# A gated linear recurrence and an ELU layer on one core: product 2 of the fast first layer and its bank's copy three products earlier, one ELU and some transfers one place later

## The chip, the core and the metric

The kernel runs on one core of a Trainium2 chip. The core has five engines that work side by side and wait for one another through semaphores: TensorE (in the profile PE, its weight loads PEld), VectorE (DVE), ScalarE (ACT), GpSimd (POOL) and SyncE (SP, which here only starts transfers). Each engine takes its instructions in the order in which the program emits them. TensorE writes its results into PSUM banks of 128x512 numbers of four bytes; DVE and ACT read them from there, and POOL cannot.

The metric is the device time of one execution in microseconds (us). Of the kernel before, three runs gave 630.42, 631.64 and 630.42 us, median 630.42 us.

## The reference

```python
def _attn_ref(q, k, v, a_re, a_im):           # each (4, 8, 768, 48)
    mag = np.sqrt(a_re * a_re + a_im * a_im)
    scale = np.minimum(mag, 0.999) / (mag + 1e-06)
    a_re_n, a_im_n = (a_re * scale, a_im * scale)
    for t in range(S):
        new_re = ar * S_re - ai * S_im        # ar, ai: row t of a_re_n, a_im_n
        new_im = ar * S_im + ai * S_re
        kv = np.einsum('bhd,bhe->bhde', k[:, :, t], v[:, :, t])
        S_re, S_im = (new_re + kv, new_im)
        y[:, :, t] = np.einsum('bhd,bhde->bhe', q[:, :, t], S_re)

def _moe_ref(x, w_in, w_out):                 # x (3072, 384), w_in (384, 2048), w_out (2048, 384)
    h = x @ w_in
    g = np.where(h > 0.0, h, np.exp(np.minimum(h, 0.0)) - 1.0)
    return g @ w_out
```

The output of the first function, with heads and their 48 columns side by side, is the `x` of the second: 4 sequences of 768 tokens, 384 columns, a hidden layer of 2048 with an ELU, and back to 384. The weights come in as double precision and are rounded on the chip.

## The kernel before

**Units.** The tokens are worked in 12 units, u = 0 to 11, each 128 tokens of two sequences. For a unit the kernel turns the gates into decays and angles (functions `squares` to `waves`), multiplies keys and queries by them (`scaled`, `gated`), transposes both, forms scores, carries the state (`small`, `masked`, `state_sums`, `valued_pe`, `carried_pe`), copies the result to `x` (`copied`, `seam`), and passes it through the two layers. Units 0 to 2 take the first layer as plain products (`inner`, `elu`); units 3 to 11 take it through a scheme with fewer products, described below. The second layer is seven products of halves (`product`) for all units from 2 on.

**The keys and queries of units 4 to 11** are turned by DVE's transpose in blocks of 32 (`flipped`, L1049) and then brought to their places by nine transfers of SP for the queries (`moved`, L1058, tile `qt<-kt`) and nine for the keys (`kt<-cs`), while POOL copies the blocks that stay on their partitions (`stayed`, L1066). The turned queries lie for that time in the tile `kt`, so the keys' transfers into `kt` come after the queries' have left it. `small` (L1221) then needs all of `kt`.

**The first layer of units 3 to 11** ("block u" below is the first layer of unit u) is 20 products p. Each is four matmuls of 128x128 by 128x128 (`mult`, L1539). In the order of TensorE:

`ORDER = 8, 1, 6, 3, 9, 7, 5, 0, 2, 14, 12, 10, 16, 18, 4, 17, 19, 13, 11, 15`

The products are summed in five PSUM banks, several after one another in the same bank: z takes 8, 1, 3, 16, 17, 15; w takes 6, 5, 14, 10, 4, 11; b takes 7; x takes 2, 12, 13; y takes 9, 0, 18, 19. Between two products of a bank its sum so far is needed, so an ACT copy (`kept`, L1552) or a DVE sum (`joint`, L1555) reads it, and the bank's next product waits for that reading:

- copy of x after product 2 into part '01' (`kept(u, '01', 'x')`): product 12 waits for it;
- copies of w after 6, 5 and 14 into '31', '30' and '10': products 5, 14 and 10 wait for them;
- copy of z after 1 into '21': product 3 waits for it; copy of x after 12 into '00': product 13;
- sum of '31' with z after product 3, and with b after product 7: product 16 waits for the first.

When a part is complete it gets its ELU: two ACT operations (`low`, L1560 and L1561), one DVE operation (`whole_of`, L1564). Part '31' is the first that is complete. While this goes on, ACT also takes two squares of a later unit's gates (`squares`, L727 and L728), DVE turns the next unit's queries and keys, and POOL multiplies that unit's keys by their gates (`gated`, L1011).

**The order of all this** is written out by hand up to unit 3 or so (the list `first`); after that every step has a due time in a plan (`put(at, fn, ...)`), and the plan is sorted by due time. Sixteen slots make a unit; the products of a block are 0.4 slots apart. The table `SHIFT` adds to a due time: an entry without `@` counts for every unit from 4 on, one with `@u` for unit u alone; in both the unit's number is left out of the name. Since an engine works in the order of emission, a shift matters only where the step passes another one of the same engine:

```python
    def put(at, fn, *args):
        at += shifted(fn, args)
```

Of the kernel before, what the change touches and what calls it, by code (L numbers as in the profile page):

```python
# [505 lines left out]
def kernel(  # L506
# [510 lines left out]
    PAIRED = 2  # L1017
# [353 lines left out]
    def folded(u, h, ks):  # L1371
        for k in ks:
            a, b, op = {
                3: (X(u, h, 0, 0), X(u, h, 1, 0), ALU.subtract),
                1: (X(u, h, 1, 0), X(u, h, 1, 1), ALU.add),
                2: (X(u, h, 1, 0), X(u, h, 0, 0), ALU.subtract),
                4: (X(u, h, 0, 1), X(u, h, 0, 0), ALU.subtract),
            }[k]
            nc.vector.tensor_tensor(out=S_of(u, k, h), in0=a, in1=b, op=op)  # L1379
# [250 lines left out]
    def warm(n):  # L1630
# [17 lines left out]
        "gated(None, ('k',))": 0.5, "gated(None, ('k',))@11": -0.3, "gated(None, ('k',))@5": -0.2,  # L1648
        "gated(None, ('q',))": 0.45, "gated(None, ('q',))@11": -0.2, "hidden(0,)": 0.05,
# [42 lines left out]
    }  # L1692

    def shifted(fn, args):

        alike = fn in (summed_in, combined, test, test_fetch) or not args
        u = 0 if alike else args[0] if type(args[0]) is int else args[-1]
        key = fn.__name__ + str(args if alike else args[1:])
        key = key.replace(repr(ALU.add), "+").replace(repr(ALU.subtract), "-")
        more = 0.0 if fn in (mult, product) or not (alike or u > PAIRED + 1) else SHIFT.get(key, 0.0)  # L1700
        return more + SHIFT.get(f"{key}@{u}", 0.0)
# [17 lines left out]
    def gates_of(u, *at):  # L1719
# [24 lines left out]
        (convert,), (waves, 1), (inner, 0, 2), (inner, 0, 0), (fetch, "in", 4), (fetch, "in", 5),  # L1744
        (load_a, 2), (table, "natural_log_exp_and_others", 1), (gated, 1, 0), (convert,),
# [12 lines left out]
        (fetch, "out", 5), *3 * [(convert,)], (load_v, 2), (powers, 2), (convert,), (elu, 1, 8),  # L1758
        (convert,), (elu, 0, 10), (convert,), (noted, 2), (ratios, 2), *3 * [(convert,)],
        (elu, 0, 14), (inner, 1, 10), *2 * [(convert,)], (elu, 0, 12), (convert,), (elu, 1, 10),  # L1760
        *4 * [(convert,)], (load_qk, 2), (convert,), (fetch, "out", 6), (project, 1, 0, 0, 4),
        (convert,), (inner, 1, 14), (slopes, 2), *3 * [(convert,)], (project, 1, 1, 0, 4),
        (project, 0, 0, 0, 4), (angles, 2), (lengths, 2), (fetch, "out", 7), (project, 0, 0, 4, 8),
        (elu, 1, 14), (project, 0, 1, 0, 4), (convert,), (decays, 2), (project, 1, 0, 4, 8),
        (carried, 2), *2 * [(convert,)], (table, "trig_and_small", 2), *2 * [(convert,)],
        (turns, 2), (waves, 2), (convert,), (table, "natural_log_exp_and_others", 2), (scaled, 2),
        (project, 0, 1, 4, 8), (convert,), (begun, 3), (convert,), (table, "trig_and_small", 3),
        (project, 0, 1, 8, 12), (convert,), (project, 1, 1, 4, 8), (squares, 3), (gated, 2),
        (project, 1, 0, 8, 12), *2 * [(convert,)], (joined, 3), (convert,), (transposed, 2, "k", 1),
        (transposed, 2, "q", 1), (convert,), (table, "natural_log_exp_and_others", 3), (convert,),  # L1770
        (ends, 2), (convert,), (logarithms, 3), (project, 1, 1, 8, 12), (powers, 3), (load_qk, 3),
        (transposed, 2, "k", 0), (convert,), (ratios, 3), (convert,), (lengths, 3),
        (project, 1, 0, 12, 16), (slopes, 3), (convert,), (transposed, 2, "q", 0),
        (project, 1, 1, 12, 16), (angles, 3), (scored, 2), (opened,), (states, 2, 0), (valued, 2),
        *3 * [(convert,)], (seam, 2), (project, 0, 0, 8, 12), (combined, 1, 1), (summed_in, 0),
        (noted, 3), (carried, 3), (summed_in, 1), (combined, 2, 1), (combined, 4, 1),
        (combined, 1, 0), (summed_in, 4), (summed_in, 2), (project, 0, 1, 12, 16), (combined, 2, 0),
        (turns, 3), (combined, 4, 0), (inner, 2, 4), (inner, 2, 6), (load_a, 4), (ends, 3),
        (inner, 2, 2), (load_v, 3), (inner, 2, 0), (elu, 2, 4), (scaled, 3), (elu, 2, 6),
        (summed_in, 3), (elu, 2, 2), (waves, 3), (gated, 3, None, ("k",)), (elu, 2, 0),  # L1780
        (gated, 3, None, ("q",)), (project, 0, 0, 12, 16), (inner, 2, 10), (transposed, 3, "k", 0),
        (warm, 2), (begun, 4), (folded, 2, 0, (3, 1)), (load_v, 4), (inner, 2, 8), (summed_in, 7),
        (squares, 4), (elu, 2, 10), (load_qk, 4), (transposed, 3, "q", 0), (transposed, 3, "q", 1),
# [154 lines left out]
```

## Time and profile before

| | |
|---|---|
| three runs, median | 630.42 us (630.42 to 631.64) |
| the profiled execution | 630.71 us |
| its span, first to last instruction | 628.9 us |
| TensorE busy | 605.8 us, 96% of the span |
| VectorE, ScalarE, GpSimd busy | 505.4, 415.0, 205.3 us |
| one product of the first layer, start to start | 0.89 us |

The span is shorter than the execution's own time by 1.81 us, which lie before the first and behind the last instruction. A row of the timeline reads: start and length in us, engine, line, operation, tile written<-tiles read, shapes, how many instructions were merged, and in brackets the idle time of the engine just before, with what ended it. A product of the first layer is eight TensorE records; its record is 1.06 us long though the next product starts 0.89 us after it, since matmuls are pipelined, so an idle time in brackets is shorter than the delay of the start.

### The profile page before, as it was taken

The page shows a single profiled execution, that of the slowest core. Times are in us where ns is not written, and L with a number is a line of the kernel's source. Part 1 is how long each engine was busy: PE and PEld are TensorE (multiplying, and loading weights), DVE is VectorE, ACT ScalarE, POOL GpSimd, SP SyncE. Part 2 cuts the span into 40 slices and gives each one's busy share as a digit, 9 for nine tenths or more (in the row PEclk, how much of TensorE's full clock was granted, in tenths as well). Part 3 has the DMA queues.
Part 4 walks back from the last instruction along what each step waited for, and adds up shares of the span by engine and source line. Part 5 has one row for each costly group of instructions (what it writes and reads, how often), then busy time and mean ns, then how long its engine had stood idle before and what let it go on. Part 6 is the DMA issues. An engine that isn't in the chain of part 4 may idle for free. (4 is left out here: it accounts for less than half of the span.)

```text
span 628.9 us, 16981 instructions
## 1 busy us (share of the span) xinstructions
PE 605.8 (96%) x6980; PEld 549.4 (87%) x6980; DVE 505.4 (80%) x789; ACT 415.0 (66%) x681; POOL 205.3 (33%) x248
## 2 busy tenths in 40 slices
PE   8889999999999999999999999999999999999996
PEld 5778886577899889999999988999999999999996
DVE  6999999877688988888888878879778877874482
ACT  6985573776868657677777776766767767661250
POOL 2010100103124624634734633634634633622000
PEclk9899999999999999999999999999999999999999
DMA  9988649541733355665565464574674675252101
GB/s 161 180 151 145 135 148 202 129 76 31 105 53 64 63 94 105 119 115 126 96 118 129 82 126 93 122 125 93 121 122 97 121 123 113 57 94 65 35 2 32
DMA packets 192179, 65.54 MB, mean 104 GB/s; under 512 B 168116, under 2 KB 181596, under 8 KB 192092
## 3 DMA queue, kind: packets, MB, share of 16 engines
q1 hardware_dynamic: 187920, 62.72, 52.1%
q0 software_dynamic: 3520, 1.20, 1.8%
q8 instruction: 57, 0.93, 0.6%
q10 hardware_dynamic: 652, 0.44, 0.3%
q14 instruction: 30, 0.25, 0.1%
HBM read 48.91 MB, written 4.80 MB: 85 GB/s over the span
## 5 line engine op out<-in xcount | busy, mean ns | idle before, releaser
L1401 PE MATMUL mlp<-w_out,g 128*128 128x192 f32 x640 | 111.9, 328 | 0.0
L1401 PEld LDWEIGHTS mlp<-w_out,g 128*128 128x128 f32 x640 | 104.3, 190 | 3.3 <-DVE ee L1415 0.6
L1123 POOL TENSOR_TENSOR S<-S,T 128x384 f32<-128x384 f32 x36 | 38.0, 1058 | 151.2 <-DVE S L1121 87.7
L1379 DVE TENSOR_TENSOR g<-g 128x512 f32<-128x512 f32 x80 | 60.7, 775 | 6.3 <-PE mlp L1401 4.7
L1292 PE MATMUL mlp<-x,w_in 128*128 128x256 f32 x288 | 64.0, 380 | 1.2 <-DMA x<-y 1.2
L1292 PEld LDWEIGHTS mlp<-x,w_in 128*128 128x128 f32 x288 | 54.2, 190 | 9.8 <-ACT n L850 1.8
L1560 ACT ACTIVATE ee<-g 128x512 f32<-128x512 f32 x63 | 39.5, 628 | 34.6 <-DVE g L1555 32.2
L1539 PE MATMUL mlp<-x,w_in 128*128 128x128 f32 x424 | 56.1, 275 | 0.0
L1272 POOL DMA_DIRECT2D x<-y x62 | 30.5, 498 | 73.6 <-ACT y L1168 41.3
L1401 PE MATMUL mlp<-w,g 128*128 128x192 f32 x320 | 54.5, 329 | 0.0
L1564 DVE SCALAR_TENSOR_TENSOR g<-ee,g 128x512 f32<-128x512 f32 x63 | 43.1, 693 | 13.1 <-ACT ee L1561 13.1
L1401 PEld LDWEIGHTS mlp<-w,g 128*128 128x128 f32 x320 | 51.8, 190 | 0.6
L1539 PEld LDWEIGHTS mlp<-x,w_in 128*128 128x128 f32 x424 | 51.6, 192 | 0.1
L1561 ACT ACTIVATE ee<-ee 128x512 f32<-128x512 f32 x72 | 45.4, 630 | 2.3
L1552 ACT COPY g<-mlp 128x512 f32<-128x512 f32 x36 | 21.0, 586 | 39.0 <-PE mlp L1539 39.0
L1555 DVE TENSOR_TENSOR g<-g,mlp 128x512 f32<-128x512 f32 x45 | 30.5, 677 | 16.1 <-PE mlp L1539 14.7
L1011 POOL TENSOR_TENSOR kg<-k,cs 128x1536 f32<-128x1536 f32 x8 | 36.9, 4614 | 1.7 <-POOL x L1522 1.4
L1539 PE MATMUL y<-x,w_in 128*128 128x128 f32 x216 | 29.4, 279 | 4.7 <-ACT g L1552 4.7
L1539 PEld LDWEIGHTS y<-x,w_in 128*128 128x128 f32 x216 | 26.2, 192 | 6.2 <-ACT g L1552 6.2
L1282 ACT ACT_TABLE_LOAD x24 | 30.8, 1283 | 0.5
L912 ACT ACTIVATE n<-w 64x384 f32<-64x384 f32 (+1 forms) x60 | 28.1, 486 | 3.9 <-PE w L897 3.0
L1539 PE MATMUL mlp<-x,g 128*128 128x128 f32 x224 | 29.7, 276 | 0.8 <-ACT g L1552 0.8
(220 smaller groups left out, 1368.0 us busy)
## 6 DMA issues: line engine op xcount, KB each, us to landing
w<-in_moe_w_out_dram SPq DMA_DIRECT2D x8, 768.0 KB, 5.9
g<-in_moe_w_in_dram SPq DMA_DIRECT2D x24, 256.0 KB, 3.7
g<-in_moe_w_out_dram SPq DMA_DIRECT2D x24, 256.0 KB, 2.8
w<-in_moe_w_in_dram SPq DMA_DIRECT2D x16, 288.0 KB, 4.8
vn<-in_v_dram SPq DMA_DIRECT2D x24, 192.0 KB, 3.8
qt<-kt SPq DMA_DIRECT2D x72, 64.0 KB, 3.4
kt<-cs SPq DMA_DIRECT2D x72, 64.0 KB, 2.5
q<-in_q_dram SPq DMA_DIRECT2D x11, 384.0 KB, 4.6
```

Of the source, the lines that this page charges most:

```text
L1011: eng.tensor_tensor(out=to.rearrange("p (h i d) -> p h i d", i=2, d=D), in0=each.unsqueeze(2).to_broadcast([C, step * H, 2, D]), in1=x["cs ...
L1123: eng.tensor_tensor(out=new_s, in0=new_s, in1=wide, op=ALU.mult)
L1272: eng.dma_start(out=x["x"][ds(j * HP + D, G), i], in_=x["y"][ds(j * HP + i * G, G)])
L1282: nc.scalar.preload_act_table_set(name)
L1292: nc.tensor.matmul(t[:, e], lhsT=w_in[:, i, ts(f + e, C)], rhs=x["x"][:, i], start=(i == 0), stop=(i == NI - 1),)
L1379: nc.vector.tensor_tensor(out=S_of(u, k, h), in0=a, in1=b, op=op)
L1401: nc.tensor.matmul(to, lhsT=a[:, m], rhs=b[:, m], start=(first and h == 0 and m == 0), stop=False, skip_group_check=True,)
L1539: nc.tensor.matmul(x["c" + c][:, ts(m, C)], lhsT=a[:, m], rhs=x["mix"][p], start=(p == BANKS[c][0] and m == 0), stop=False, skip_group_che ...
L1555: nc.vector.tensor_tensor(out=part(u, to), in0=part(u, a), in1=part(u, b), op=op)
L1560: nc.scalar.activation(out=e, in_=part(u, of), func=AF.Relu, scale=-1.0)
L1561: nc.scalar.activation(out=e, in_=e, func=AF.Exp, scale=-1.0)
L1564: nc.vector.scalar_tensor_tensor(out=part(u, to), in0=nat[u]["e", to], scalar=-1.0, in1=part(u, of), op0=ALU.add, op1=ALU.max,)
```

## The change

Nothing is computed differently; steps change places.

- **Product 2** in blocks 4 to 11 gets a shift of -1.2 slots: TensorE's order becomes 8, 1, 6, 3, 9, 7, **2**, 5, 0, 14, 12, 10 and on as before. To allow this, `shifted` now takes entries for `mult`.
- **The copy of bank x** into '01' gets -1.2 slots too: ACT's order in blocks 4 to 11 was copy '30', ELU of '31', copy '01', copy '10'; it becomes copy '01', copy '30', ELU of '31', copy '10'.
- **The sums and the ELU of '31'** get +0.4 slots in blocks 4 to 11 (one product). On DVE only one step passes another: the sum for '20' (reads bank y after product 0) now comes before the last step of the ELU of '31'.
- **In block 3** the copy '10' of bank w comes before the two squares of unit 5 on ACT, not behind them; the product order stays.
- **The queries' turning and transfers** get +0.3 slots: on DVE the last sum of the second layer (`product(u, 3, 1)`, L1427) now comes before the first of the two transposes, not between them. On SP nothing passes anything, except in block 9 (transfers of unit 10), where a shift of 2 slots puts one check fetch of a weight (`test_fetch`, 256 KB) ahead of the queries' nine transfers; on POOL the sum `joined` of unit 11 comes before unit 10's `stayed` queries there.
- **Early in the program** (the list `first`): the load of unit 2's gates comes before the fetch of a part of `w_in`, not behind it, on SP; and the two notes of unit 2 (`noted`, L807) come before two exponentials and two ELUs on ACT, not behind them.

```diff
@@ SHIFT
+        "flipped('q', 0)": 0.3,  "flipped('q', 1)": 0.3,
-        "joint('31', '31', 'z', -)": -0.5,
+        "joint('31', '31', 'b', +)": 0.4,  "joint('31', '31', 'z', -)": -0.1,
-        "kept('10', 'w')@3": 0.2,
+        "kept('01', 'x')": -1.2,
+        "load_a()@10": 0.05,
+        "low('31', '31')": 0.4,
-        "moved('k', 0)@10": 0.6,
+        "moved('k', 0)@10": 2.6,
+        "moved('q', 0)": 0.3,  "moved('q', 1)": 0.3,  "moved('q', 2)": 0.3,
+        "moved('q', 0)@10": 2,  "moved('q', 1)@10": 2,  "moved('q', 2)@10": 2,
+        "stayed('q',)@10": 2,
+        "mult(14,)@3": -0.2,  "mult(2,)": -1.2,
+        "whole_of('31', '31')": 0.4,  "whole_of('31', '31')@4": 0.3,
@@ shifted
-        more = 0.0 if fn in (mult, product) or not (alike or u > PAIRED + 1) else SHIFT.get(key, 0.0)
+        more = SHIFT.get(key, 0.0) if alike or u > PAIRED + 1 else 0.0
@@ first
-        ... (fetch, "in", 4), (fetch, "in", 5), (load_a, 2), ...
+        ... (fetch, "in", 4), (load_a, 2), (fetch, "in", 5), ...
-        ... (load_v, 2), (powers, 2), (convert,), (elu, 1, 8), (convert,), (elu, 0, 10), (convert,), (noted, 2), (ratios, 2), ...
+        ... (noted, 2), *2 * [(convert,)], (load_v, 2), (powers, 2), (convert,), (elu, 1, 8), (convert,), (elu, 0, 10), (convert,), (ratios, 2), ...
```

The diff is put together here by entry; in the file the table is sorted by name, so most of its lines move. The shifts of the keys' transfer of unit 10, of `load_a` and of product 14 in block 3 change no engine's order by themselves.

More of the change, by code (lines that the diff above doesn't have):

```diff
@@ L1642 @@
         "ends()@3": -0.5, "ends()@4": 0.1, "flipped('k', 0)": 0.3, "flipped('k', 0)@4": 0.1,
[5 rows of a table removed]
-        "gated(None, ('k',))": 0.5, "gated(None, ('k',))@11": -0.3, "gated(None, ('k',))@5": -0.2,
-        "gated(None, ('q',))": 0.45, "gated(None, ('q',))@11": -0.2, "hidden(0,)": 0.05,
[16 rows of a table removed]
[5 rows of a table added]
+        "folded(1, (4,))@5": -0.7, "gated()": 0.05, "gated(None, ('k',))": 0.5,
+        "gated(None, ('k',))@11": -0.3, "gated(None, ('k',))@5": -0.2, "gated(None, ('q',))": 0.45,
[19 rows of a table added]
         "powers()@5": -0.5, "pronounced()": 2.8, "ratios()": 0.2, "ratios()@3": 0.5,
@@ L1743 @@
         (table, "trig_and_small", 1), (convert,), (seam, 0), (convert,), (warm, 1), (turns, 1),
-        (convert,), (waves, 1), (inner, 0, 2), (inner, 0, 0), (fetch, "in", 4), (fetch, "in", 5),
-        (load_a, 2), (table, "natural_log_exp_and_others", 1), (gated, 1, 0), (convert,),
+        (convert,), (waves, 1), (inner, 0, 2), (inner, 0, 0), (fetch, "in", 4), (load_a, 2),
+        (fetch, "in", 5), (table, "natural_log_exp_and_others", 1), (gated, 1, 0), (convert,),
         (gated, 1, 1), (convert,), (elu, 0, 2), (convert,), (transposed, 1, "q", 0),
@@ L1757 @@
         (fetch, "out", 4), (inner, 0, 10), (inner, 0, 14), (elu, 1, 12), (inner, 0, 12), (convert,),
[L1758 to L1780, printed above, removed]
@@ L1781 @@
-        (gated, 3, None, ("q",)), (project, 0, 0, 12, 16), (inner, 2, 10), (transposed, 3, "k", 0),
-        (warm, 2), (begun, 4), (folded, 2, 0, (3, 1)), (load_v, 4), (inner, 2, 8), (summed_in, 7),
-        (squares, 4), (elu, 2, 10), (load_qk, 4), (transposed, 3, "q", 0), (transposed, 3, "q", 1),
+        (fetch, "out", 5), (convert,), (noted, 2), *2 * [(convert,)], (load_v, 2), (powers, 2),
+        (convert,), (elu, 1, 8), (convert,), (elu, 0, 10), (convert,), (ratios, 2),
+        *3 * [(convert,)], (elu, 0, 14), (inner, 1, 10), *2 * [(convert,)], (elu, 0, 12),
@@ new lines @@
+        (convert,), (elu, 1, 10), *4 * [(convert,)], (load_qk, 2), (convert,), (fetch, "out", 6),
+        (project, 1, 0, 0, 4), (convert,), (inner, 1, 14), (slopes, 2), *3 * [(convert,)],
+        (project, 1, 1, 0, 4), (project, 0, 0, 0, 4), (angles, 2), (lengths, 2), (fetch, "out", 7),
+        (project, 0, 0, 4, 8), (elu, 1, 14), (project, 0, 1, 0, 4), (convert,), (decays, 2),
+        (project, 1, 0, 4, 8), (carried, 2), *2 * [(convert,)], (table, "trig_and_small", 2),
+        *2 * [(convert,)], (turns, 2), (waves, 2), (convert,),
@@ new lines @@
+        (table, "natural_log_exp_and_others", 2), (scaled, 2), (project, 0, 1, 4, 8), (convert,),
+        (begun, 3), (convert,), (table, "trig_and_small", 3), (project, 0, 1, 8, 12), (convert,),
+        (project, 1, 1, 4, 8), (squares, 3), (gated, 2), (project, 1, 0, 8, 12), *2 * [(convert,)],
+        (joined, 3), (convert,), (transposed, 2, "k", 1), (transposed, 2, "q", 1), (convert,),
+        (table, "natural_log_exp_and_others", 3), (convert,), (ends, 2), (convert,),
+        (logarithms, 3), (project, 1, 1, 8, 12), (powers, 3), (load_qk, 3), (transposed, 2, "k", 0),
@@ new lines @@
+        (convert,), (ratios, 3), (convert,), (lengths, 3), (project, 1, 0, 12, 16), (slopes, 3),
+        (convert,), (transposed, 2, "q", 0), (project, 1, 1, 12, 16), (angles, 3), (scored, 2),
+        (opened,), (states, 2, 0), (valued, 2), *3 * [(convert,)], (seam, 2),
+        (project, 0, 0, 8, 12), (combined, 1, 1), (summed_in, 0), (noted, 3), (carried, 3),
+        (summed_in, 1), (combined, 2, 1), (combined, 4, 1), (combined, 1, 0), (summed_in, 4),
+        (summed_in, 2), (project, 0, 1, 12, 16), (combined, 2, 0), (turns, 3), (combined, 4, 0),
@@ new lines @@
+        (inner, 2, 4), (inner, 2, 6), (load_a, 4), (ends, 3), (inner, 2, 2), (load_v, 3),
+        (inner, 2, 0), (elu, 2, 4), (scaled, 3), (elu, 2, 6), (summed_in, 3), (elu, 2, 2),
+        (waves, 3), (gated, 3, None, ("k",)), (elu, 2, 0), (gated, 3, None, ("q",)),
+        (project, 0, 0, 12, 16), (inner, 2, 10), (transposed, 3, "k", 0), (warm, 2), (begun, 4),
+        (folded, 2, 0, (3, 1)), (load_v, 4), (inner, 2, 8), (summed_in, 7), (squares, 4),
+        (elu, 2, 10), (load_qk, 4), (transposed, 3, "q", 0), (transposed, 3, "q", 1),
```

80 rows, old and new, of the table SHIFT are left out of this document.

## The prediction

> **What bounds the kernel now.** I read the page first, then the list of who waited for whom on TensorE, then the chain of waits, then the timeline of one block. The page and the waits:
>
> ```profile
> span 628.9 us, 16981 instructions
> PE 605.8 (96%) x6980; PEld 549.4 (87%) x6980; DVE 505.4 (80%) x789; ACT 415.0 (66%) x681; POOL 205.3 (33%) x248
> kt<-cs SPq DMA_DIRECT2D x72, 64.0 KB, 2.5
> ```
>
> ```profile
> PE y L1539 <- ACT g L1552: 4.7, 8, 1.2
> ```
>
> TensorE is the bound with 96%, so only its idle places and what delays its starts can be won. The largest of them is this row: a first-layer product into bank x or y waited eight times for an ACT copy, once in each block from 3 to 10. The chain of waits shows how block 8 came to it:
>
> ```profile
> 449.17 5.00 POOL kg L1011
> ...
> 456.64 0.64 ACT ee L1560
> 457.30 0.63 ACT ee L1561
> 457.93 0.48 ACT g L1552
> ```
>
> POOL gates the next unit's keys for 5.00 us; DVE turns them; only then can DVE add bank b to part '31'; ACT takes the ELU of '31'; and behind the ELU in ACT's order stands the copy of bank x. TensorE's own rows in this block (8 records are one product; in the old order product 8 is at 448.95):
>
> ```profile
> 449.84 1.06 PE L1539 MATMUL mlp<-halves,g 128*128 128x128 f32 x8
> 450.74 1.06 PE L1539 MATMUL mlp<-x,w_in 128*128 128x128 f32 x8
> 451.63 1.10 PE L1539 MATMUL mlp<-halves,g 128*128 128x128 f32 x8
> 452.57 1.06 PE L1539 MATMUL y<-x,w_in 128*128 128x128 f32 x8
> ...
> 456.14 1.06 PE L1539 MATMUL y<-x,more 128*128 128x128 f32 x8
> 457.04 1.06 PE L1539 MATMUL mlp<-x,w_in 128*128 128x128 f32 x8
> 458.46 1.16 PE L1539 MATMUL y<-x,w_in 128*128 128x128 f32 x8 [0.36 <-ACT g L1552]
> 459.45 1.06 PE L1539 MATMUL mlp<-x,g 128*128 128x128 f32 x8
> ```
>
> The pitch is 0.89 us. Product 2 starts at 456.14, 14 at 457.04; 12 should start at 457.93 and starts at 458.46, 0.53 late; product 10 then comes 0.99 after it, 0.10 over the pitch. So a bracket of 0.36 stands for 0.63 us: the idle time plus 0.27, of which 0.17 shows in the waiting product's own start and 0.10 in the next. The other large waits:
>
> ```profile
> 268.24 1.16 PE L1539 MATMUL y<-x,w_in 128*128 128x128 f32 x8 [1.17 <-ACT g L1552]
> 363.09 1.16 PE L1539 MATMUL y<-x,w_in 128*128 128x128 f32 x8 [0.97 <-ACT g L1552]
> 505.38 1.16 PE L1539 MATMUL y<-x,w_in 128*128 128x128 f32 x8 [0.65 <-ACT g L1552]
> ```
>
> These are blocks 4, 6 and 9. Block 3 (rows below) has 0.42 of the 4.7; what is left for blocks 5, 7, 8 and 10 is 4.7 - 0.42 - 1.17 - 0.97 - 0.65 = 1.5, or 0.37 each.
>
> **Product 2 and its copy, blocks 4 to 11.** *Removed:* product 12's wait in seven blocks (block 11 has none: nothing is turned there any more). Price with 0.27 each: 1.44 + 1.24 + 0.92 + 4 x 0.64 = 6.2 us. The copy of x now runs beside product 5, four products before 12 needs it.
>
> *New wait 1:* product 14 now comes two products after 5 instead of three, and waits for the copy '30'. The same spacing is in the rows above and on ACT here:
>
> ```profile
> 450.94 0.58 ACT L1552 COPY g<-mlp 128x512 f32<-128x512 f32 x1 [0.61 <-PE mlp L1539]
> 453.06 0.83 ACT L728 ACTIVATE n<-ai 128x768 f32<-128x768 f32 x1
> ```
>
> Product 1 starts at 449.84, its copy at 450.94 (1.10 later) and ends at 451.52; product 3, two products later, starts on time at 451.63, but the one behind it comes 0.94 after it, 0.05 over. ACT is free from 453.89 on. So I take 0.05 for each of 8 blocks, 0.4 us; the bounds are 0 and, for a start that misses by as much as product 12's did here with its restart, 0.63 each or 5 us; the rows of product 3 are the nearest.
>
> *New wait 2:* the copy '10' still stands behind the ELU of '31', so it now runs in the ACT slot that copy '01' had, and product 10 waits for it. Product 12 was late by its idle time plus 0.17; product 10 is due one product later, so it is late by idle + 0.17 - 0.89: block 4 0.45, block 6 0.25, block 9 and the rest below zero. With 0.10 for the restart that is 0.55 + 0.35 = 0.9 us. In block 8 the margin is thin: the copy '30' now ends about 456.93 (product 5 at 455.25 + 1.10 + 0.58), so the ELU starts 0.3 later than 456.64, copy '10' ends about 458.8, and product 10 is due at 458.83. The bound is 0 to 0.1 in each of five blocks; I take 0. DVE gains a little: the sum for '20' fills the time in which it would wait for the ELU.
>
> Up to the end of the product stage the sum is 6.2 - 0.4 - 0.9 = 4.9 us.
>
> **What is late next: the keys.** The scores (L1221) that follow each block need the keys' nine transfers, which hang on POOL and DVE and not on the products. Whatever TensorE wins before them it can lose there. The keys' transfers of blocks 4, 5 and 8, the scores after them, and the check fetch behind block 9's queries:
>
> ```profile
> L1058 SPq DMA_DIRECT2D kt<-cs x9: 585/630/1746, 270.8 to 277.3; - x9
> 279.82 2.42 PE L1221 MATMUL y<-qt,kt 96*64 96x64 f32 x64
> L1058 SPq DMA_DIRECT2D kt<-cs x9: 585/627/637, 317.1 to 322.5; - x9
> DMA to landing us min/median/max: 2.1/2.5/4.3
> 327.10 2.05 PE L1221 MATMUL y<-qt,kt 96*64 96x64 f32 x62 [0.32 <-DMA vn<-in_v_dram]
> L1058 SPq DMA_DIRECT2D kt<-cs x9: 585/627/1216, 460.5 to 466.5; - x9
> 470.04 2.39 PE L1221 MATMUL y<-qt,kt 96*64 96x64 f32 x64
> 505.69 0.53 SPq L687 DMA_DIRECT2D g<-in_moe_w_out_dram  x1
> 517.81 1.40 PE L1221 MATMUL y<-qt,kt 96*64 96x64 f32 x39
> ```
>
> In block 4 the last transfer starts at 277.3; with the page's median of 2.5 it lands at 279.8, and the scores start at 279.82: no slack. In block 5 the scores already stop once, for 0.32; the row names another transfer that shares the semaphore, but the longest keys' landing there, 4.3 after 322.5, is 326.8, just ahead of the restart at 327.10. So what these two win in their products, 1.44 - 0.55 - 0.05 = 0.84 and 0.64 - 0.05 = 0.59, I count as lost. In block 8 the slack is 470.04 - 466.5 - 2.5 = 1.0 us against 0.59 won, so it stays; blocks 6, 7 and 10 I take like it. The queries' transfers keep their start: DVE ends both transposes at the same time, only the sum between them comes first. In block 9 the check fetch goes first; it costs the queries 0.5 of issue and the keys as much or, with the landing of 256 KB, up to 2; its scores start 517.81, long behind, so I take 0. The sum is 4.9 - 0.84 - 0.59 = 3.5 us.
>
> The Trainium skill, page "DMA: Bandwidth & Descriptors", section "Anatomy of one DMA", fits a transfer's time as 2.0 us plus its bytes over 436 KB per us. By that, as an estimate, 64 KB land 2.15 us after the issue, block 5's keys at 324.7, and its 0.59 would be kept: 626.3 instead of the forecast. The trace's 4.3 in block 5 speaks against it, since other transfers run then.
>
> **Block 3.** The first stall stays; the second goes:
>
> ```profile
> 217.63 0.84 ACT L727 ACTIVATE n<-ar 128x768 f32<-128x768 f32 x1
> 217.78 1.16 PE L1539 MATMUL y<-x,w_in 128*128 128x128 f32 x8 [0.42 <-ACT g L1552]
> 219.73 1.16 PE L1539 MATMUL mlp<-x,g 128*128 128x128 f32 x8 [0.79 <-ACT g L1552]
> 224.28 1.16 PE L1539 MATMUL mlp<-halves,w_in 128*128 128x128 f32 x8 [0.71 <-DVE g L1555]
> 229.94 2.44 PE L1221 MATMUL y<-qt,kt 96*64 96x64 f32 x64 [0.74 <-DMA kt<-cs]
> ```
>
> Copy '10' ahead of the squares frees product 10 by 0.79 + 0.27 = 1.06 us. But product 17 waits for DVE at 224.28, and the scores wait for the keys at 229.94, which nothing here brings sooner. I take 0; the bounds are 0 and, if the keys came early too, 1.06 less.
>
> **The early edits.** Both lie under TensorE's unbroken run:
>
> ```profile
> 67.70 28.22 PE L1292 MATMUL mlp<-x,w_in 128*128 128x256 f32 x130
> 89.36 0.92 ACT L807 ACTIVATE n<-n,most_sq 128x768 f32<-128x768 f32 x1
> 52.53 5.13 SPq L611 DMA_DIRECT2D ai<-in_a_im_dram  x1
> ```
>
> The notes (about 2 us of ACT) delay two ELUs by that, and three banks in turn cover it. The load's 5.13 us on SP now stand ahead of a weight fetch, whose weights this run of TensorE uses only later than the fetch's landing. I take 0 for both; without the cover it would be 2 us on the one and up to 5 on the other, and a gain has no place there, since the run has no gap.
>
> **The sum.** Against the profiled execution: span 628.9 - 3.5 = 625.4, and with 1.81 around it 627.2 against 630.71. The median of the runs, 630.42, is 0.29 below that execution, so the forecast is 626.9 us.
>
> **Rivals.** *The keys don't bind in blocks 4 and 5* (queries' sum ahead, so the queue is emptier): 4.9 us won, 625.5. For it: median landings of 2.5; against it: block 5 waits now. *The keys bind everywhere:* were they 1 us later in blocks 6, 7, 8 and 10, only block 9's 0.87 would be left: 629.6, same. Against it: 1.0 us of slack in block 8. *Slower: the later landing spreads.* TensorE and DVE ahead of time let the fetches behind the keys start sooner, and every block's keys land as slowly as block 5's, 4.3 after the issue. Block 8's scores then start at 466.5 + 4.3 + 0.2 = 471.0, 1.0 late instead of 0.6 early; block 4's at 281.8, 2.0 late. With 1.0 each in blocks 6, 7, 8 and 10 and 2.0 in 4, less 0.9 from block 9, that is 5.1 lost: 635.5. It decides from landings of 3.5 on; only one block of eight shows one. *The wait only changes its place,* all of it to product 10: excluded by one product's 0.89 us, except in blocks 4 and 6.
>
> **How the numbers follow.** Forecast 0.6; keys not binding in 4 and 5, 0.2; keys bind everywhere 0.12; slower 0.08. A measurement can tell 0.2%, 1.26 us, from no change. Faster is the first two together, 0.8; same 0.12; slower 0.08. The range reaches from 625.0 (keys free and no new wait in part) to 629.6.
>
> **What would show it.** In the changed profile: no bracket on product 12 in blocks 4 to 10; short ones on product 10 in blocks 4 and 6; the waits of L1539 into y down from 4.7 to about 0.4; waits of L1221 for transfers of 0.5 to 0.9 in blocks 4 and 5; block 10 ending its products 0.6 sooner after its start. The prediction is wrong if product 10 waits in most blocks, if the scores wait in blocks 6 to 10, or if block 9's keys land behind its scores' due time.

## The result and the profile after

Nine executions of the changed kernel gave a median of 627.14 us (622.94 to 633.97), nine of the kernel before, on the same chip, 630.42 us (628.93 to 634.08). The ratio is 0.9931, with a 95% interval from 0.9901 to 0.9960: faster by 0.4 to 1.0%. A later comparison of the same two kernels gave 0.9959 (0.9933 to 0.9985). Some executions run slow (here those more than 1.5% above the fastest of their kernel): the medians include them, every ratio leaves them out, and the one profile of such an execution is left out of the table of blocks below. The profiled execution took 627.64 us, its span 625.8.

The page after (busy time of the engines; the keys' transfers with their median from issue to landing), and who waited for whom on TensorE (us in total, times, longest):

```profile
PE 605.9 (97%) x6980; PEld 551.1 (88%) x6980; DVE 509.0 (81%) x789; ACT 415.9 (66%) x681; POOL 203.8 (33%) x248
...
kt<-cs SPq DMA_DIRECT2D x72, 64.0 KB, 2.3
```

```profile
PE y L1221 <- DMA kt<-cs: 3.5, 1, 3.5
PE w L1106 <- issue: 1.8, 2, 1.2
...
PE mlp L1539 <- ACT g L1552: 0.4, 1, 0.4
PE y L1539 <- ACT g L1552: 0.4, 1, 0.4
```

The eight waits of 4.7 us are one of 0.4, which is block 3's, where product 12 kept its place. In their stead stands one wait that was 0.7 before: 3.5 us before one set of scores. TensorE's timeline of block 8, products 0, 14, 12, 10, 16 in turn:

```profile
454.92 1.06 PE L1539 MATMUL y<-pair,w_in 128*128 128x128 f32 x8
455.81 1.10 PE L1539 MATMUL mlp<-x,w_in 128*128 128x128 f32 x8
456.75 1.06 PE L1539 MATMUL y<-x,w_in 128*128 128x128 f32 x8
457.65 1.10 PE L1539 MATMUL mlp<-x,g 128*128 128x128 f32 x8
458.59 1.06 PE L1539 MATMUL mlp<-x,w_in 128*128 128x128 f32 x8
```

Product 12 follows 14 without a stop. What is left of the two new waits in this block is 0.05 behind 14 and 0.05 behind 10 (0.94 to the next start, where 0.89 is the pitch).

Block 3 is where the changed kernel lost. First TensorE's timeline, then SP's, then TensorE's busy time and granted clock by stretches of 3.4 us (the columns are the stretch, its length, busy time and count of PE, PEld, DVE, ACT and POOL, the granted clock, the DMA share and GB/s):

```profile
224.59 1.15 PE L1106 MATMUL w<-vn,kg 64*64 64x48 f32 x64
229.26 4.04 PE L1221 MATMUL y<-qt,kt 96*64 96x64 f32 x64 [3.52 <-DMA kt<-cs]
233.23 2.08 PE L1539 MATMUL mlp<-pair,w_in 128*128 128x128 f32 x8
```

```profile
216.60 5.44 SPq L1058 DMA_DIRECT2D kt<-cs  x6
222.13 0.56 SPq L684 DMA_DIRECT2D g<-in_moe_w_in_dram  x1
222.74 1.06 SPq L607 DMA_DIRECT2D vn<-in_v_dram  x2
223.90 2.72 SPq L1058 DMA_DIRECT2D kt<-cs  x3
```

```profile
225.00:228.40 3.40, 0.74 (x52) 0.62 (x44) 2.86 (x6) 2.14 (x4) 0.00 (x0) 1.00 1.06 170
228.40:231.80 3.40, 2.54 (x42) 2.47 (x44) 2.54 (x4) 2.10 (x5) 0.00 (x0) 0.50 0.16 50
231.80:235.20 3.40, 3.40 (x37) 3.28 (x34) 0.00 (x0) 0.32 (x1) 0.00 (x0) 0.50 0.00 0
235.20:238.60 3.40, 3.40 (x66) 3.17 (x68) 3.26 (x6) 2.51 (x4) 0.83 (x1) 0.99 0.00 0
```

The products end 1.8 us sooner after the block's start, the keys do not land sooner, and TensorE is idle for 3.52 us. Then its granted clock is 0.50 for two stretches, and scores that took 2.44 us take 4.04, product 15 takes 2.08 for 1.16.

One profile of each kernel would mislead here, as the next table shows. It has the length of each block, from its first product to the first of the next (for block 11 to the end of the span), in the profiled executions of the five kernels in which product 2 stands as before, and of eight in which it stands as changed; the kernels are those of the next section (all but the one with keys first and the scores behind product 15 only).

| block | product 2 as before | median | as changed | median | difference | forecast |
|---|---|---|---|---|---|---|
| 4 | 46.81 to 47.47 | 47.20 | 46.10 to 46.59 | 46.44 | -0.77 | 0 |
| 5 | 46.63 to 46.92 | 46.74 | 46.10 to 46.98 | 46.41 | -0.33 | 0 |
| 6 | 49.04 to 49.38 | 49.10 | 48.14 to 50.47 | 48.42 | -0.68 | -0.84 |
| 7 | 46.98 to 47.26 | 46.99 | 46.92 to 47.20 | 47.20 | +0.21 | -0.59 |
| 8 | 46.63 to 46.66 | 46.66 | 46.10 to 46.48 | 46.10 | -0.56 | -0.59 |
| 9 | 46.46 to 46.49 | 46.47 | 45.64 to 45.67 | 45.64 | -0.82 | -0.87 |
| 10 | 44.49 to 44.51 | 44.50 | 43.97 to 44.00 | 43.99 | -0.51 | -0.59 |
| 11 | 42.16 to 42.47 | 42.35 | 42.17 to 42.51 | 42.33 | -0.02 | +0.05 |

The differences sum to -3.5 us, as forecast. In block 7 the median jumps between two lengths 0.27 apart, which both orders show; the means are 47.09 and 47.10. Block 3 starts anywhere between 206.5 and 214.1 us in these thirteen executions; most of the scatter of a whole execution comes from there and from block 3.

### The profile page after: what moved, and what is told of

It is laid out like the page before. It is cut to its first block, busy times and chain, and to the rows that moved or that the text cites. A ratio compares the mean times of both kernels' runs of the same rounds, so it can differ in the third digit from the quotient of the medians.

```text
span 625.8 us, 16976 instructions
## 1 busy us (share of the span) xinstructions
PE 605.9 (97%) x6980; PEld 551.1 (88%) x6980; DVE 509.0 (81%) x789; ACT 415.9 (66%) x681; POOL 203.8 (33%) x248
## 5 line engine op out<-in xcount | busy, mean ns | idle before, releaser
L1539 PE MATMUL mlp<-x,w_in 128*128 128x128 f32 x424 | 56.6, 276 | 0.0
L1564 DVE SCALAR_TENSOR_TENSOR g<-ee,g 128x512 f32<-128x512 f32 x63 | 49.2, 789 | 4.2 <-ACT ee L1561 4.2
L1539 PEld LDWEIGHTS mlp<-x,w_in 128*128 128x128 f32 x424 | 51.5, 192 | 0.3
L1552 ACT COPY g<-mlp 128x512 f32<-128x512 f32 x36 | 21.0, 585 | 25.6 <-PE mlp L1539 25.3
L1539 PE MATMUL mlp<-x,g 128*128 128x128 f32 x224 | 30.1, 277 | 0.1
L1259 ACT COPY x<-y 128x384 f32<-128x384 f32 x20 | 8.6, 482 | 31.4 <-PE y L1151 31.4
L1539 PE MATMUL y<-x,w_in 128*128 128x128 f32 x216 | 28.6, 275 | 0.4 <-ACT g L1552 0.4
```

The lines of the kernel that those rows point to most:

```text
L1539: nc.tensor.matmul(x["c" + c][:, ts(m, C)], lhsT=a[:, m], rhs=x["mix"][p], start=(p == BANKS[c][0] and m == 0), stop=False, skip_group_che ...
L1564: nc.vector.scalar_tensor_tensor(out=part(u, to), in0=nat[u]["e", to], scalar=-1.0, in1=part(u, of), op0=ALU.add, op1=ALU.max,)
```

## The experiments

Each was timed in five rounds beside the kernel before; ratios are to that kernel, with 95% intervals. In the three comparisons that kernel gave 631.57, 631.78 and 631.44 us, while the expectations start from 630.42; so a measured time is set against them by its ratio, 1.0 to 1.4 us lower than it stands.

### Does product 2 alone carry the gain? And the queries' moves?

```diff
 (the kernel before; shifted takes entries for mult)
+        "kept('01', 'x')": -1.2,  "mult(2,)": -1.2,
+        "joint('31', '31', 'b', +)": 0.4,  "low('31', '31')": 0.4,  "whole_of('31', '31')": 0.4,  "whole_of('31', '31')@4": 0.3,
-        "joint('31', '31', 'z', -)": -0.5,
+        "joint('31', '31', 'z', -)": -0.1,
```

> The kernel before with one part of the change: in blocks 4 to 11 product 2 and the copy of bank x get -1.2 slots and the sums and ELU of '31' +0.4. Theory A, this part carries the whole gain of the later blocks and needs nothing of the queries' moves: the blocks 4 to 10 shorten by what they do in the changed kernel (1.3, 0.8, 0.9, 0.1, 0.5, 0.8, 0.5, together 4.9), block 3 stays as before (scores 0.74 late, 2.44 long), so 625.5 to 626. Theory B, the keys bind in blocks 4 and 5 unless the queries' sum is moved too: 0.84 and 0.59 of it stay lost, scores there wait 0.5 to 0.9 for keys, 626.9 to 627.5. No part of it: 630.4.

Measured: 628.34 us, 0.9938 (0.9907 to 0.9968), which is as much as the whole changed kernel gains (0.9931 and 0.9959). Block 3 is as before, 49.73 us, and the wait of L1539 for copies into y is down to block 3's 0.4. In block 5 its scores wait once:

```profile
330.42 0.30 PE L1221 MATMUL y<-qt,kt 96*64 96x64 f32 x2
331.28 2.05 PE L1221 MATMUL y<-qt,kt 96*64 96x64 f32 x62 [0.56 <-DMA g<-in_moe_w_in_dram]
```

The transfer that the row names shares a semaphore; the keys' own last landing there is at 330.9. The ratio makes 626.5 of 630.42, between the times of theories A and B, and its interval holds both. The blocks decide: in this profile 4 to 10 are 4.1 shorter than in the profile before, without the queries' moves (theory A), and theory B's wait is there too, in block 5 with 0.56. The part holds three steps (product 2, its copy, the sums and ELU of '31'); which of them is needed, and whether the copy alone ahead of that ELU would do, was not tested.

```diff
 (the kernel before)
+        "flipped('q', 0)": 0.3,  "flipped('q', 1)": 0.3,
+        "moved('q', 0)": 0.3,  "moved('q', 1)": 0.3,  "moved('q', 2)": 0.3,
+        "moved('q', 0)@10": 2,  "moved('q', 1)@10": 2,  "moved('q', 2)@10": 2,
+        "stayed('q',)@10": 2,  "moved('k', 0)@10": 2.6,  "load_a()@10": 0.05,
```

> The kernel before with only the queries' turning and transfers moved back (and in block 9 one check fetch ahead of them). Theory A (the prediction's): worth nothing by itself, 630.4, blocks 4 to 10 as long as in the kernel before, product 12's eight waits stay. Theory B: the queries' move empties the queue and lets the keys of blocks 4 and 5 land 0.5 to 1 earlier after the block's start than 20.1 to 21.7 and 21.0 to 21.4 us, so part of the changed kernel's gain in these two is its doing. Theory C: the fetch ahead of block 9's queries makes that block's scores late: block 9 longer than 46.5.

Measured: 631.89 us, 1.0028 (1.0000 to 1.0055). Blocks 4 to 10 are as long as in the unchanged kernels (47.20, 46.66, 49.26, 46.99, 46.66, 46.49, 44.50), and the waits stay: `PE y L1539 <- ACT g L1552` has 4.4 us in 8. Keys land no sooner: 20.74 and 21.10 us after the start of blocks 4 and 5, where four executions without the move have 20.1 to 21.7 and 21.0 to 21.4. Theory A; the moves are worth nothing by themselves, or cost a little.

### The early edits

```diff
 (load_alone: the kernel before)
-        (fetch, "in", 4), (fetch, "in", 5), (load_a, 2),
+        (fetch, "in", 4), (load_a, 2), (fetch, "in", 5),
```

> The kernel before with unit 2's gates loaded ahead of the fetch of a part of w_in, and nothing else. Theory A: this is what took TensorE's unexplained wait of 1.05 us at 63.1 us away (its own instructions' transfer ran at 60.0 among the loads): that wait is gone, block 3 starts 1.1 us earlier, and by then the keys, which don't come earlier by as much, take some or all of it back: 629.3 to 630.4. Theory B: the wait has nothing to do with the load (it comes from the other early edit or comes and goes): the wait stays, 630.4.

```diff
 (notes_alone: the kernel before)
-        (fetch, "out", 5), *3 * [(convert,)], (load_v, 2), ... (elu, 0, 10), (convert,), (noted, 2), (ratios, 2),
+        (fetch, "out", 5), (convert,), (noted, 2), *2 * [(convert,)], (load_v, 2), ... (elu, 0, 10), (convert,), (ratios, 2),
```

> The kernel before with the two notes of unit 2 ahead of two exponentials and two ELUs on ACT, and nothing else. Theory A (as in the prediction): covered by TensorE's unbroken run, 630.4 +- 0.5, block 3 starts at 208.2. Theory B: part of block 3's start 1.6 us earlier in the changed kernel is from here: block 3 starts up to 1.6 earlier, time 628.8 to 630.4. A loss of up to 2 us if the ELUs behind the notes are not covered: 632.

Measured: 630.27 us, 0.9979 (0.9951 to 1.0008), and 631.3 us, 0.9990 (0.9962 to 1.0018). Neither can be told from no change. The wait of TensorE at 63 us, which is gone in the changed kernel's first profile, is gone with the load moved, gone in a kernel that did not move it, and long in one that did (the timelines of the kernel with the load alone, of the one with block 3's copy alone, and of the last but one of this section):

```profile
60.37 1.28 PE L1106 MATMUL w<-vn,kg 64*64 64x48 f32 x64
```

```profile
60.97 1.15 PE L1106 MATMUL w<-vn,kg 64*64 64x48 f32 x64
```

```profile
62.25 1.14 PE L1106 MATMUL w<-vn,kg 64*64 64x48 f32 x63
65.81 0.24 PE L1106 MATMUL w<-vn,kg 64*64 64x48 f32 x1 [2.42 <-issue]
```

So theory B: it comes and goes, between 0 and 2.7 us, and the 1.6 us by which block 3 started sooner in the changed kernel's profile lie within that scatter.

### Block 3: the copy, alone and undone

```diff
 (the kernel before)
-        "kept('10', 'w')@3": 0.2,
```

> The kernel before with the copy '10' of block 3 ahead of the two squares, and nothing else. The scores behind block 3 wait for the keys in any case. Theory A (as in the prediction: the wait only grows): products 1.0 to 1.8 shorter, the wait before the scores 0.74 + 1.8 = 2.5, the scores as long as before (2.44), time 630.4 +- 0.5. Theory B (TensorE's idle time itself costs clock, from well under 3.5 us on): scores 4.0 instead of 2.4 and the product behind them 2.1 instead of 1.2, 632 to 633. Between them: the clock falls only from an idle time of more than 2.5 on, then it reads as theory A here although the changed kernel, with 3.5, loses.

Measured: 632.67 us, 1.0022 (0.9987 to 1.0056). Block 3's products are 2.0 shorter and the block 51.7 long, where the six kernels that leave it alone have 49.7 to 50.3. The timeline and the stretches:

```profile
229.41 2.94 PE L1221 MATMUL y<-qt,kt 96*64 96x64 f32 x64 [3.19 <-DMA kt<-cs]
```

```profile
224.20:227.60 3.40, 2.01 (x73) 1.77 (x71) 2.49 (x6) 2.69 (x5) 0.00 (x0) 1.00 1.09 189
227.60:231.00 3.40, 1.54 (x44) 1.46 (x46) 2.61 (x6) 2.10 (x5) 0.00 (x0) 1.00 0.40 91
231.00:234.40 3.40, 3.40 (x36) 3.28 (x33) 0.65 (x2) 1.02 (x2) 0.00 (x0) 0.51 0.00 0
```

Idle 3.19 us, and the clock is half for 3.4: not theory A. Since the idle time came out at 3.19 and not at 2.5, this run does not tell theory B from a clock that falls only from more than 2.5 on. By times alone the loss is not shown, since the interval holds 1.

```diff
 (the changed kernel)
+        "kept('10', 'w')@3": 0.2,
```

> The changed kernel with block 3's copy '10' put back behind the two squares. The scores behind block 3 wait for the keys until the same time, but TensorE comes to them later, so that its idle time before them falls from 3.5 to 1.5 to 2.5. Theory A, an idle time of 3 and more halves TensorE's granted clock for some us: the clock stays at 1.0 between 228 and 236, scores 2.4 instead of 4.0, block 3 2.0 to 2.9 shorter, 624.3 to 625.2. Theory B, the clock falls for another cause (it fell there by chance, or the earlier products as such): no difference, 627.1.

Measured: 627.23 us, 0.9941 (0.9913 to 0.9969): by time no different from the changed kernel, against theory A's 2 to 2.8 us less. In its profile block 3 is as theory A says, 50.3 us, its scores at full clock after a short wait; but block 6 is 2.0 longer than in the changed kernel's, because TensorE was idle there for 1.56 us, which nothing in the profile ended, and the clock fell behind that:

```profile
229.48 2.39 PE L1221 MATMUL y<-qt,kt 96*64 96x64 f32 x64 [1.11 <-DMA kt<-cs]
...
376.41 1.03 PE L1106 MATMUL w<-vn,kg 64*64 64x48 f32 x40 [1.56 <-issue]
```

```profile
373.40:376.80 3.40, 1.84 (x82) 1.68 (x80) 1.38 (x2) 2.21 (x4) 0.83 (x1) 1.00 0.19 34
376.80:380.20 3.40, 3.40 (x37) 3.31 (x29) 2.71 (x5) 0.00 (x0) 0.83 (x1) 0.50 0.09 16
```

Theory A holds for the mechanism in block 3. One profile does not say why the median gained nothing; what the edit is worth on the mean of many executions stays open within 2 us.

```diff
 (the changed kernel, no edit)
```

> The changed kernel itself once more, timed beside the two kernels that mend block 3 in it. All theories: 0.993 of the time before, within its interval. Whether block 3 loses again is the question: if the idle time before its scores halves the clock each time it is 3 us and more, block 3 is 53 +- 0.7 us long again, with the clock at 0.5 for some 3.4 to 7 us; if it was chance, nearer 50.

Measured: 629.07 us, 0.9959 (0.9933 to 0.9985). Block 3 is 51.7 long: idle 3.0 before the scores, the clock 0.50 from 230.9 to 234.3. So the idle time comes back; the length of the fall differs (6.8 us the first time, 3.4 here). In block 5 of this execution the scores wait for 0.88 us:

```profile
328.26 2.05 PE L1221 MATMUL y<-qt,kt 96*64 96x64 f32 x62 [0.88 <-DMA vn<-in_v_dram]
```

### Mending block 3

```diff
 (the changed kernel)
-        "moved('k', 2)@4": 4.2,
+        "moved('k', 2)@4": 3.4,
```

> The changed kernel with the third part of unit 4's keys' transfers (three of nine) ahead of one check fetch and of the load of unit 5's values on SP, which took 0.56 + 1.06 us there. Theory A: SP's order holds these keys; they land 1.7 earlier, the idle time before block 3's scores falls from 3.5 to 1.8, the clock does not fall, block 3 is 1.7 + 2.5 shorter: 622.5 to 623.5. Theory B: DVE's turning or POOL's gating holds them, SP would only wait: they land when they did, 627.1, and the values come later.

Measured: 630.49 us, 0.9980 (0.9953 to 1.0007). Neither theory: the keys' last transfer lands at 227.2, 18.4 us after the block's start and no longer 22.9, and yet the scores start at 231.45. TensorE's row and DVE's:

```profile
231.45 2.92 PE L1221 MATMUL y<-qt,kt 96*64 96x64 f32 x64 [3.41 <-DVE g L1555]
```

```profile
229.13 0.42 DVE L698 TENSOR_REDUCE seen<-g 128x1 f32<-128x256 f32 x1 [3.24 <-DMA g<-in_moe_w_in_dram]
...
230.66 0.68 DVE L1555 TENSOR_TENSOR g<-y,g 128x512 f32<-128x512 f32 x1
```

The scores are written into bank y, so they also wait for DVE's last sum with y (230.66 + 0.68 = 231.34). In front of that sum DVE has a check of a weight (`test`, L698), which waits for its fetch; the fetch now stands behind the keys. In the changed kernel this check held DVE too, for 1.45 us, and the sum ended at 227.7, hidden behind the keys, for which the scores waited until 229.26.

```diff
 (the changed kernel: the scores behind product 15 and a second-layer product)
-        "small()@4": -0.7,
+        "small()@4": -0.15,
```

> The changed kernel with unit 4's scores behind product 15 of block 3 and the first product of halves of the second layer, not before them. These take 0.93 + 2.8 us of TensorE. Theory A: they fill the idle time of 3.5, the keys land meanwhile, no idle time and no fall of the clock: 3.5 + 2.5 won, up to 621 to 622. Theory B: the second-layer product waits for the ELU of its part in place of the scores for their keys, TensorE is idle as long, and the scores and all that hangs on them come later by 2.8: 627 to 630.

Measured: 623.71 us, 0.9889 (0.9853 to 0.9924), 623.4 of 630.42. Theory A, though the time is 1.4 above its range: of the second-layer product only the first eight matmuls (1.47 us) stand ahead of the scores, and 0.85 of idle time is left. Block 3 is 47.8 long, and the granted clock is 1.00 through the span up to its last 1.4 us:

```profile
226.40 1.06 PE L1539 MATMUL mlp<-pair,w_in 128*128 128x128 f32 x8
227.29 1.47 PE L1401 MATMUL mlp<-w_out,g 128*128 128x192 f32 x8
228.69 1.15 PE L1106 MATMUL w<-vn,kg 64*64 64x48 f32 x64
230.69 2.44 PE L1221 MATMUL y<-qt,kt 96*64 96x64 f32 x64 [0.85 <-DMA kt<-cs]
```

```diff
 (the changed kernel: keys first, and the scores behind product 15 only)
-        "moved('k', 2)@4": 4.2,  "small()@4": -0.7,
+        "moved('k', 2)@4": 3.4,  "small()@4": -0.55,
```

> The changed kernel with both: the third part of unit 4's keys ahead of the check fetch and the values on SP, and unit 4's scores behind product 15 of block 3 (not behind the second-layer product). If SP's order holds the keys, 1.7 of the idle time of 3.5 goes to the earlier landing and 0.9 to product 15; 0.9 is left, the clock does not fall: 621.5 to 623. If SP's order does not hold them, 2.6 of idle time stays, near the length from which the clock falls: 624 to 626.

Measured: 628.47 us, 0.9940 (0.9910 to 0.9970), 626.6 of 630.42 and so above both ranges that were expected. Its profile shows what the kernel with the keys first showed: TensorE is again idle before the scores, 3.36 us, until DVE's sum with y.

```diff
 (the changed kernel)
-        "moved('k', 2)@4": 4.2,
+        "moved('k', 2)@4": 3.4,
     clear = [x for x in clear if x > 58]
+    clear[0] = 59.4
```

The entry of `clear` is the due time of the first check on DVE; it was 58.6, ahead of the sum of '30' with y.

> The changed kernel with the third part of unit 4's keys ahead of the check fetch and the values on SP, as before, and now the first check of a weight (a DVE reduction that waits for the fetch) behind the sums of '30' and '10', not before the sum of '30' with bank y, for which the scores wait as well. Theory A, the keys' place on SP alone held the scores: no better than the kernel with the keys first, block 3 at 52.2, 630. Theory C, two things end at nearly the same time, the keys' landing (SP's order) and DVE's last reading of bank y (held 1.5 to 3.2 us by the check): with both out of the way TensorE waits 0.7 or less, the clock stays at 1.0, block 3 is 47.5 to 48.5 long and not 53.2, and the time is 622 to 623.

Measured: 623.35 us in only six executions, 0.9878 (0.9833 to 0.9924), 622.7 of 630.42. Theory C. Block 3 is 47.4 long; the check stands behind the sum, and the scores start 0.11 after the sum's end (232.81 + 0.68):

```profile
232.81 0.68 DVE L1555 TENSOR_TENSOR g<-y,g 128x512 f32<-128x512 f32 x1
...
234.74 0.41 DVE L698 TENSOR_REDUCE seen<-g 128x1 f32<-128x256 f32 x1
```

```profile
233.60 2.39 PE L1221 MATMUL y<-qt,kt 96*64 96x64 f32 x64 [0.46 <-DVE g L1555]
```

```diff
 (the same, and)
-        "small()@4": -0.7,
+        "small()@4": -0.55,
```

> The same with unit 4's scores behind product 15 of block 3. Theory C: product 15 covers the rest of the wait, block 3 is 47.0 to 47.8 long, 621.5 to 622.5, at most 0.7 better than without it and within what can be told from the kernel with the scores behind a second-layer product (0.989 of the time before). If the scores' own followers (masks, carried state) are late now, 0 to 1 worse.

Measured: 623.91 us, 0.9884 (0.9857 to 0.9911), block 3 47.1 long, no wait before its scores. The three mended kernels cannot be told from one another. The last two were timed beside the changed kernel and beat it by 0.8% (0.9878 and 0.9884 against 0.9959, intervals apart), some 4.9 us, where their block 3 is 4.3 to 4.6 us shorter than in the changed kernel's profile of that comparison. The first of the three was not timed beside it.

The granted clock, which is on record for every timed execution, points the same way without a profile. Taken as time times (1 - clock), the mean over the executions that count in the ratios, the clock took 4.3 to 6.4 us where block 3's copy is early and its scores still wait (four kernels, the changed one in both its comparisons), 3.1 to 3.2 in the three mended ones, and 2.7 to 4.4 in those that leave block 3 alone; the ranges just touch.

## Why the prediction was right, and where only the sum was

**The time: right, and in part by luck.** The forecast for the blocks was kept in the sum and not in each block. Block 3 and its start, for which nothing was forecast, moved as much: between the two profiled executions blocks 4 to 11 won 4.95 us, block 3 lost 3.51, and its start came 1.65 sooner, together the 3.1 by which the span is shorter.

**Product 12's waits: right.** They are gone in blocks 4 to 10, and one part of the change alone (0.9938) gains as much as the whole.

**New wait 1: right,** 0.05 for each block, the row of product 3 that it was taken from. **New wait 2: right in block 6, mis-sized in block 4.** In block 6 product 10 starts 1.11 after 12 and product 16 0.99 after 10, together 0.32 late against 0.35 forecast:

```profile
361.78 1.06 PE L1539 MATMUL y<-x,w_in 128*128 128x128 f32 x8
362.89 1.16 PE L1539 MATMUL mlp<-x,g 128*128 128x128 f32 x8
```

In block 4 the two starts come 0.94 and 0.99 after the one before, 0.15 late instead of 0.55, and 0.05 to 0.44 in the eight executions of the table. The step carried product 12's old wait of 1.17 over from one execution; the other four profiles with the old order have 0.55 to 1.04 there. In blocks 5 and 7 to 10 0.05 is there, within the bounds of 0 to 0.1.

**The keys in blocks 4 and 5: half wrong.** They were to take all that the products of these blocks win. By the medians the products are 0.92 and 0.53 shorter and the blocks 0.77 and 0.33, so the keys took at most 0.15 and 0.20. The step that failed is "no slack" in block 4, read from one execution; with the new order the scores there wait for the keys in two of eight executions, for 0.26 and 0.24. Another execution of that unchanged stretch (the kernel with the load alone) shows the last transfer issued at 274.6 and the scores at 278.29, 3.7 later, so with the median landing of 2.5 a slack of 1.2:

```profile
L1058 SPq DMA_DIRECT2D kt<-cs x9: 585/628/1141, 268.7 to 274.6; - x9
```

```profile
278.29 0.93 PE L1221 MATMUL y<-qt,kt 96*64 96x64 f32 x15
```

In block 5 the last landing lies behind the scores' due time in six of the eight executions, and four of these show waits of 0.43 to 0.88 (two of them in rows above), so there the reading of the 4.3 us landing was right in kind. The Trainium skill, "DMA: Bandwidth & Descriptors", section "Anatomy of one DMA — SWDGE (gpsimd) path", has a fit by which, as an estimate, these 64 KB would land 2.15 us after the issue; it was made on transfers that GpSimd issues, and these are SP's. The median of 2.3 in the profile after agrees with it nearly, and block 5's late landings do not.

**Blocks 6, 8, 9, 10: right** to 0.2 by the medians. Block 9's scores kept their slack behind the check fetch. In block 8 the slack was enough in seven executions of eight; in the changed kernel with block 3's copy put back the keys landed 20.9 us after the block's start, when the scores were due at 20.55, and the block is 0.38 longer:

```profile
469.38 2.05 PE L1221 MATMUL y<-qt,kt 96*64 96x64 f32 x62 [0.42 <-DMA kt<-cs]
```

**Block 7: wrong.** Its products are 0.53 shorter, and the block is not. Its timeline after the change:

```profile
421.57 2.05 PE L1221 MATMUL y<-qt,kt 96*64 96x64 f32 x62 [0.19 <-issue]
423.55 1.02 PE L1106 MATMUL w<-vn,kg 64*64 64x48 f32 x53
425.21 0.43 PE L1106 MATMUL w<-vn,kg 64*64 64x48 f32 x11 [0.65 <-issue]
```

In and behind the scores TensorE is idle for 0.19 and 0.65, which nothing in the profile's work ends; before, the second was 0.27 and the first absent, and TensorE went on 24.74 us after the block's start, now 24.69. The forecast had no term for such a wait. Against the forecast it took 0.8 away by the medians, and blocks 4 and 5 brought 1.1 that were not counted on: the sum of the blocks was right by two errors of opposite sign.

**Block 3: wrong in sign.** "I take 0; the bounds are 0 and 1.06 less" left out a loss, although the text said that the keys would not come sooner. It follows that the idle time grows by what the products save (from 0.74 to 3.0 and 3.5), and such an idle time has a price of its own, the clock. Where that copy is moved and nothing is mended, block 3 is 51.7 to 53.2 long (three profiles), 1.6 to 3.1 more than its median of 50.1 without; where the scores' needs are mended too, it is 47.1 to 47.8, 2.3 to 3.0 less than that median. The times alone do not show the loss: the changed kernel and the one with its block 3 put back have the same ratio within the intervals.

**The early edits: not told from the forecast's 0.** The intervals reach from 3.1 us less to 0.5 more for the load, and from 2.4 less to 1.1 more for the notes.

**The rivals.** "Keys don't bind in 4 and 5" was nearer to block 4 than the forecast. "Keys bind everywhere" and "the landing spreads" did not happen: blocks 6, 9 and 10 have no wait before their scores, and block 8 has one in one execution of eight. That the wait would only change its place was excluded for the products except in blocks 4 and 6, and rightly; it did change its place in block 3, to the keys.

## What to carry to other kernels

Where work is brought forward in front of something that does not come sooner, the idle time there grows, and where it takes up half of a 3.4 us window or more it can also cost clock: either bring the late thing forward too, or put other work of the same engine into the gap. Before a wait is mended, list everything that the waiting instruction needs, here the keys' landing and the last reading of its bank: mending the one that the row names only uncovers the other, and moved the check that held it still later. Slack and lateness of a few tenths read from one profile are scatter until a second execution has shown them.

## What the runs showed of the hardware that was not expected

**The clock is granted in windows of 3.41 us.** Wherever the granted clock changes within a profiled execution, it does so on a grid of that pitch, whose phase differs from one execution to the next, and a stretch at half clock is 3.41 or 6.83 us long (the last one, at the end of the span, apart). Between 60 and 615 us it matters how busy TensorE was in the window before. After five windows with 0.34 to 1.2 us busy of 3.4 the next was at 0.50, each time; after 2.0 and more it never was. Between, it went both ways: at half after windows with 1.54, 1.61, 1.62 and 1.84, at full after 1.73 and 1.88. Before 45 us busy time does not tell: the clock stayed after windows with 1.5 to 1.6 us busy and fell after some with 2.3 to 3.1. So the condition stays open. What the idle times show: from 60 us on, all eight of 2.4 to 3.5 us had a window at half clock within or behind them, one of 1.56 had, and one of 1.53 had not; two of 2.3 and 2.5 at 45 us had none. A window at half clock costs up to 1.7 us of TensorE's work (half of 3.41).

The Trainium skill, "TensorE: Matmul & The Clock Gate", Part 1, tells of a free-running window of about 3.4 us and of half clock after an idle window. The runs agree with the window's length and differ in the condition: a window that was idle for little less than half was sometimes enough.

**TensorE seems to wait for its own instructions, and by chance.** The same place at 63 us cost 0 to 2.7 us in executions of like kernels, and a second one in block 6 up to 1.56, with a fall of the clock behind three of the long ones (2.70, 2.42 and 1.56 us). In the fourteen profiles, each of the 36 idle times of TensorE of 0.5 us or more after 15 us that nothing in the profile's work ends lies the same way: TensorE goes on 1.2 to 1.8 us after the end of a 16 KB packet of the queue that the profile calls instruction. That speaks for late instructions; no run moved that queue. The 0.19 in block 7 has no such packet before it, and its cause is open. Executions of one kernel differ by 0.8 to 1.8%; between the profiled ones, these waits, what the clock takes behind them, and block 3 are among the largest differences. What makes an instruction transfer late was not settled; moving one load out of its way showed no effect on the time.
